# The third chunk of x with seven block products: V's first tile and kv first, sums and low parts earlier

## The chip, the core and the metric

The kernel runs on one core of a Trainium2 chip. The engines have queues of their own, which run in program order and meet only through semaphores: TensorE (PE in the profile) multiplies, VectorE (DVE), ScalarE (ACT) and GpSimd (POOL) work on elements, and SyncE (SP) issues most of the DMAs. The metric is the device time of one execution in microseconds; several executions are timed and their median is taken. A second, profiled execution gives the trace.

## What is computed

x is 2048 x 512. Two branches work on it and a gate mixes them:

```python
g = sigmoid((x * gate_w).sum(-1, keepdims=True))
q, k, v = split_heads(x @ wqkv)                      # 32 heads of 16
phi(u)  = concat(softmax(u @ w_phi), softmax(-(u @ w_phi)))
kv, z   = phi(k)^T v, sum over rows of phi(k)
a = (phi(q) kv / (phi(q) z + 1e-6)) @ wo
b = mish(x @ w1 + b1) @ w2
out = g * a + (1 - g) * b
```

All is float32.

## The kernel before, in words

Every float32 operand of TensorE is split into a high part, rounded to the multiplier's format (a copy on ScalarE), and a low part, the rest (a subtraction on VectorE or GpSimd). A product then takes three matmuls: high by high, high by low, low by high.

**Stage A** goes through x in 8 chunks of 256 rows (c = 0 to 7, two tiles of 128 rows each). w_phi is multiplied into the weights of q and k first, so a chunk needs six products of 128 x 512 by 512 x 512: k, v and q of two tiles. Each is 12 matmuls (4 along the 512, times 3). The chunk gives phi(k), which VectorE and ScalarE make, kv is summed up in PSUM from phi(k) and v, and q goes to DRAM. **Stage B** then goes through 4 blocks of 512 rows with both branches; the two matrices of the Dense branch are loaded and split during stage A.

In the chunks of `FAST` (c = 3, 4, 5 before) the four products for k and q are made as a 2 x 2 block product in Strassen's manner (in Winograd's form): seven products of half the length, s1 to s7, of 6 matmuls each, in place of eight. It needs four sums of the weights, t1, t3, t2 and t4 (made once, from the raw weights, and split: steps h0 to h3 for the high parts, l0 to l3 for the low parts, numbered in this order), and four sums of quarters of x for each such chunk, step `sa` (four additions on GpSimd), split by `sh0`, `sh1` (ScalarE) and `sl0`, `sl1` (GpSimd). s7 takes the first sum of x and t3, s6 the second and t2, s5 the third and t1, s3 the fourth and a block of wq; s1, s2 and s4 take x itself. The pieces meet so: `bc` copies s1's result to a second PSUM tile (ScalarE), on which s6, s5 and s3 accumulate; `m7` copies s7's (ScalarE); `ca` adds m7 to that tile (VectorE) and starts the tile of k of the second 128 rows, on which s4 accumulates; `qa` makes q of the second tile (VectorE). So s4 waits for ca, ca for s6 and m7, and s6 for bc.

Other steps, by the names in the lists: `xh`, `xl` split the next chunk's x (ScalarE, VectorE); `ldx` loads the chunk after that one; `mx`, `mn` are the row maxima and minima of k per head, `d0`, `d1` the two differences, `E` the exponential, `S` its sums, `rS` their reciprocal, `ml` the scaled E = phi(k) (all on VectorE but E); a digit behind them is the tile. `ve` copies v out, `qe` q; `st` stores q. `z` adds phi(k) to a sum in DRAM by a DMA that GpSimd issues (directly on GpSimd from c = 5 on). `kk` is the kv product of two chunks (128 small matmuls), `kv` of one. `H`, `O`, `L` are the split (high, low) of a piece of the Dense branch's weights and the load of a later piece; `O` is on GpSimd.

The order is written out by hand, as a list of steps for each chunk (FIRST, SECOND, BEFORE, SEVEN, NEXT, LAST); a mark behind a name means the previous chunk ('), the next (+), or a step of the weights (#). Each engine runs its own instructions in the order of these lists. `behind(ins)` adds a wait: the GpSimd instruction starts only when VectorE's step noted last (`dve[0]`: an `xl`, an `ml`) is done. Buffers rotate: the raw x and the sums of x share two tiles (`tx`), k's PSUM tiles three (`a`), the others four (`dn`), v's tiles four (`io`).

In the list BEFORE, for chunk 2, the order on TensorE is k0, kk, k1, v0, v1, q0, q1. In SEVEN it is s1, s7, s2, (kk,) s6, v0, s4, s5, v1, s3; in the first of these chunks v1 and s3 stand ahead of E1. `run` reads a list. A step that has been run is gone from the table, so a name that comes a second time does nothing.

Of the kernel before, what the change touches and what calls it, by code (L numbers as in the profile page):

```python
# [12 lines left out]
ALU = mybir.AluOpType  # L13
# [18 lines left out]
GROW = FA % P  # L32
ORDER = [NFA - 1] + list(range(NFA - 1)) + list(range(NFA, NF))
WARM = 6
FAST = range(3, 6)

# [3 lines left out]
    S0 rS0 ml0 S1 rS1 ml1 q0 qe0 st0 q1 qe1 st1  # L42
"""
SECOND = """
    h0# h1# l0# z0' z1' k0 mx0 mn0 d00 d10 ldx k1 E0 L0# L1# xh mx1 mn1 d01 d11 v0 E1 S0 rS0 ve0 ml0 xl z0
    v1 S1 rS1 ml1 ve1 q0 qe0 st0 q1 qe1 st1 t2#
"""
BEFORE = """
    z1' xh xl k0 kk h3# l1# mx0 mn0 d00 d10 k1 E0 sa ldx sh0 sl0 sh1 sl1 h2# mx1 mn1 d01 d11 v0 E1 H0# O0# L2# l2# S0 rS0 ve0 ml0 z0
    v1 H1# S1 rS1 ml1 l3# O1# L3# ve1 q0 qe0 st0 q1 qe1 st1  # L50
"""
SEVEN = """
    s1 bc ve1' s7 m7 sh1' sl1' s2 kk xh xl zld sa z1' more mx0 s6 ca mn0 d00 d10 E0 ldx v0 ve0 sh0 sl0 za rest S0 rS0 s4 s5 qa st1 mx1 mn1 d01 d11 E1 ml0 late
# [41 lines left out]
def tile_gated_mix(ctx: ExitStack, tc: tile.TileContext, xT, wv, wkT, wqT, bd, w1a, w1b, b1, w2a, w2b, wo, out):  # L95
# [6 lines left out]
    pin = tc.keep_in_program_order  # L102
    SYNC = mybir.DependencyInfo(mybir.DependencyClass.Sync, mybir.DependencyReason.DATA)
    V, G_, A_, Sy = nc.vector, nc.gpsimd, nc.scalar, nc.sync
# [11 lines left out]
    def k4(name, tag, dt=F32):  # L116
        return T([P, 1024], dt, tag, {"E": 4, "tx": 2, "oh": 2, "z": 1}[tag], name)
# [8 lines left out]
    def act(out_, in_, fn=AF.Copy, **k):  # L126
        return pin(A_.activation(out_, in_, fn, **k))  # L127

    def kt(t, f):
        return t[:, : KT * f].rearrange("p (k f) -> p k f", f=f)  # L130
# [4 lines left out]
    def f32(ap):  # L135
        return ap.bitcast(F32)
# [65 lines left out]
    def at(key, name, fn):  # L202
        steps.setdefault((key, name), []).append(fn)

    def run(text, key, prev=None, nxt=None):
        for w in text.split():
            k = prev if w.endswith("'") else nxt if w.endswith("+") else "W" if w.endswith("#") else key
            for fn in steps.pop((k, w.rstrip("'+#")), ()):
                fn()
# [4 lines left out]
    xs, Es, vs, psA, low = {}, {}, {}, {}, {}  # L214
# [41 lines left out]
    def feat_ops(key, t, src, d, negative=False):  # L256

        n = str(t)

        def red(name, op):  # L260
            d[name] = T([P, H], F32, name, 2, name)
            pin(V.tensor_reduce(d[name], hv(src()), axis=AX.X, op=op))

        def dd(a):
            if "E" not in d:
                d["E"] = k4("E", "E")
            E = hv(d["E"][:, a * 512 : (a + 1) * 512])
            if (a == 0) != negative:
                pin(V.tensor_sub(E, hv(src()), d["mx"][:, :, None].to_broadcast([P, H, DH])))
            else:  # L270
                ins = pin(V.tensor_sub(E, d["mn"][:, :, None].to_broadcast([P, H, DH]), hv(src())))  # L271
                if key[0] == "B":
                    dve[0] = ins

        def ss():
            d["S"] = T([P, 2 * H], F32, "Sm", 2, "Sm")
            pin(V.tensor_reduce(d["S"], hv(d["E"][:, :]), axis=AX.X, op=ALU.add))  # L277

        at(key, "mx" + n, lambda: red("mx", ALU.max))
        at(key, "mn" + n, lambda: red("mn", ALU.min))  # L280
        at(key, "d0" + n, lambda: dd(0))
        at(key, "d1" + n, lambda: dd(1))
        at(key, "E" + n, lambda: act(d["E"], d["E"], AF.Exp))
        at(key, "S" + n, ss)
        at(key, "rS" + n, lambda: pin(V.reciprocal(d["S"], d["S"])))

    dve = {}

    def behind(ins, other=None):
        tc.add_manual_dep(ins.ins, (other or dve[0]).ins.name, SYNC, reason="VectorE's step first")  # L290

    def scale_by(d, eng):
        dve[0] = pin(eng.tensor_mul(hv(d["E"][:, :]), hv(d["E"][:, :]), d["S"][:, :, None].to_broadcast([P, 2 * H, DH])))  # L293
# [6 lines left out]
    SX = [t[:, 1024:2048].rearrange("p (i k f) -> p i k f", i=4, k=2) for t in TS]  # L300
    SR = []

    def tops():

        k0, k1, q0, q1 = raw = [x[:, i : i + 2, :] for x in (wkr, wqr) for i in (0, 2)]
        t1, t4, t3, t2 = raw
        hl = [(*(x[:, i, :, :] for i in range(3)), y) for x, y in zip(TT, T4)]
        at("W", "t1", lambda: pin(G_.tensor_sub(t1, k0, q0)))
        at("W", "t3", lambda: pin(G_.tensor_sub(t3, q1, q0)))
        at("W", "t4", lambda: pin(G_.tensor_sub(t4, q1, k1)))  # L310
        at("W", "t4", lambda: pin(G_.tensor_add(t4, t4, t1)))
        at("W", "t2", lambda: pin(V.scalar_tensor_tensor(t2, t1, -1.0, q1, op0=ALU.mult, op1=ALU.subtract)))
        for i, r in enumerate((t1, t3, t2, t4)):
            at("W", f"h{i}", lambda i=i, r=r: act(hl[0][i], r))
            if i in (1, 3):
                at("W", f"l{i}", lambda i=i, r=r: behind(pin(G_.tensor_sub(hl[1][i], r, f32(hl[0][i])))))
            else:
                at("W", f"l{i}", lambda i=i, r=r: pin((V if i else G_).tensor_sub(hl[1][i], r, f32(hl[0][i]))))
        return list(zip(*hl))

    (t1, t3, t2, t4) = tops()
    wk0, wk1, wq1 = (wkh[:, :2, :], wkl[:, :2, :]), (wkh[:, 2:, :], wkl[:, 2:, :]), (wqh[:, 2:, :], wql[:, 2:, :])

    def kt4(t):
        return [t[:, o : o + 512].rearrange("p (i k f) -> p i k f", i=2, k=2) for o in (0, 512)]

    def fast_operands(c, key):

        def sa():
            SR[:] = kt4(k4("sraw", "tx"))  # L330
            r = kt(rawx[c], SC)
            a11, a12, a21, a22 = [r[:, k : k + 2, t * P : (t + 1) * P] for t in range(2) for k in (0, 2)]
            (s3, s2), (s1, s4) = [[x[:, i, :, :] for i in range(2)] for x in SR]
            for o, a, b in ((s1, a21, a22), (s3, a11, a21), (s2, a11, s1), (s4, a12, s2)):
                ins = pin(G_.tensor_add(o, a, b))
                if o is s1:
                    behind(ins, low[c])

        at(key, "sa", sa)
        for j in range(2):  # L340
            sl = slice(2 * j, 2 * j + 2)
            at(key, f"sh{j}", lambda j=j, sl=sl: act(SX[0][:, sl, :, :], SR[j]))
            at(key, f"sl{j}", lambda j=j, sl=sl: pin(G_.tensor_sub(SX[1][:, sl, :, :], SR[j], f32(SX[0][:, sl, :, :]))))

    def fast_ops(c, key, P_):

# [47 lines left out]
    def a_ops(c):  # L394
        key = ("A", c)
        P_ = psA[c] = {}
        for t in range(2):
# [28 lines left out]
            at(key, f"v{t}", v_)  # L426
            if c not in FAST:
                at(key, f"k{t}", k_)
                at(key, f"q{t}", q_)
            at(key, f"ve{t}", ve)  # L430
            if t and c in FAST:
                at(key, "qa", qa)
            else:
                at(key, f"qe{t}", qe)
            at(key, f"st{t}", st)
            feat_ops(key, t, lambda t=t: P_["k", t][:, :], d, t == 1 and c in FAST)
            at(key, f"ml{t}", lambda d=d: scale_by(d, V))

            def zs(t=t, d=d):
                if c >= FAST[-1]:  # L440
                    for sl in (slice(0, 512), slice(512, 1024)) if t and c == NCH - 1 else (slice(0, 1024),):
                        behind(pin(G_.tensor_add(Z["acc"][:, sl], Z["acc"][:, sl], d["E"][:, sl])))
                elif c:
                    pin(G_.dma_start(zd[t][:, :], d["E"], accum_op=ALU.add))
                else:
                    pin(G_.dma_start(zd[t][:, :], d["E"]))

            at(key, f"z{t}", zs)
        if c == FAST[-1]:
            def zld():  # L450
                Z["acc"] = k4("zacc", "z")
                pin(Sy.dma_start(Z["acc"], zd[0][:, :]))
# [17 lines left out]
        odd = c + 1 - c % 2  # L470
        if c <= FAST[-1]:
            at(("A", odd + 1), "kk", kv)
# [4 lines left out]
        if c + 1 in FAST:  # L477
            fast_operands(c + 1, key)
# [13 lines left out]
    W = {}  # L492
# [349 lines left out]
    for j in range(2):  # L842
        h, l = [w[:, 2 * j : 2 * j + 2, :].rearrange("p k f -> p (k f)") for w in (wvh, wvl)]
# [12 lines left out]
    for i in range(4):  # L856
        j, r = i // 2, i % 2
# [13 lines left out]

    run(FIRST, ("A", 0))
    run(SECOND, ("A", 1), ("A", 0))
    run(BEFORE, ("A", 2), ("A", 1))
    for c in FAST:
        w = {3: ("", "H2# O2# L4# H3#", "O3# L5# z0"), 4: ("", "H4# O4# L11# H5#", "O5# L7# z0"), 5: ("H11# O11# L8# H7# O7# L9#", "", "H8# O8# L6#")}[c]
        text = SEVEN
        for name, part in zip(("more", "rest", "late"), w):
            text = text.replace(name, part)
        if c == FAST[0]:  # L880
            text = text.replace("E1 ml0", "v1 s3 qe0 st0 E1 ml0").replace("v1 S1 rS1 s3 ve1 qe0 st0 ml1", "S1 rS1 ml1")
        run(text, ("A", c), ("A", c - 1))
    for c, text in ((NCH - 2, NEXT), (NCH - 1, LAST)):
        run(text, ("A", c), ("A", c - 1), ("B", 0))
# [63 lines left out]
```

## Time and profile before

| | |
|---|---|
| median of 3 runs | 449.17 us (449.09 to 449.27) |
| the profiled execution: its time, and its span | 449.46 us, 447.7 us |
| TensorE's granted clock | 1.0 |
| chunk 2 on TensorE (k0 to q1) | 46.66 to 65.13 us |
| chunk 3 on TensorE (s1 to s3) | 65.13 to 80.09 us |
| stage A ends, stage B begins | 149.4 us |

How the profile is read: a row of the timeline has the start in us from the span's start, the duration in us, the engine, the line of the program, the operation, the tiles (written <- read, by the program's names without buffer numbers), their sizes, the count that is merged in the row, and in brackets the time the engine had waited just before, with what ended the wait. Many rows have line 107 (every matmul) or 127 (every ScalarE copy), since helpers issue them; so the tiles tell the steps apart: `proj<-w2ah,w2bh` is a block product of sums (s7, s6 or s5), `proj<-w2bh,xh` is s4, since the weights' sums lie in tiles named w2a and w2b until the Dense branch's weights take their place. The sums of x have the name `sraw`, and their split lies in w2bh and w2bl. A matmul's recorded duration overlaps that of the next one; start to start tells the pace.

### The profile page before, as it was taken

What the parts mean: (1) busy time and instruction counts of PE and PEld (TensorE: products, weight loads), DVE (VectorE), ACT (ScalarE), POOL (GpSimd) and SP (SyncE); (2) the same over time, 40 slices, a digit from 0 to 9 for tenths busy, and PEclk for the clock granted to TensorE, in tenths of its full rate; (3) what the DMA queues carried; (4) which work ended last, traced back from release to release, by engine and by line L of the source; (5) the groups of instructions that cost most, each with busy time, mean ns of one, the idle gap of its engine ahead of it and who ended that gap; (6) DMA issues with size and microseconds to landing.
All of it is one profiled execution on the core that took longest, in us unless ns stands there. A gap on an engine that the chain in (4) does not pass through costs nothing.

```text
span 447.7 us, 7013 instructions
## 1 busy us (share of the span) xinstructions
PE 441.1 (99%) x2754; PEld 360.8 (81%) x2754; DVE 318.5 (71%) x423; ACT 209.4 (47%) x289; POOL 157.7 (35%) x116
## 2 busy tenths in 40 slices
PE   7999999999999999999999999999999999999996
PEld 7888888888888888787787887887887888787885
DVE  2499787988999999699979867386967529701002
ACT  4774454464545746426365443634253544233220
POOL 2296657775558263312022221113212123221211
PEclk9999999999999999999999999999999999999999
DMA  7426746869934200405352141321141302030002
GB/s 281 167 66 220 145 120 162 209 145 267 289 135 130 72 24 14 128 9 130 111 156 69 48 141 47 93 97 47 42 147 49 88 7 94 1 89 7 0 0 94
DMA packets 27320, 46.35 MB, mean 104 GB/s; under 512 B 5908, under 2 KB 14100, under 8 KB 27288
## 3 DMA queue, kind: packets, MB, share of 16 engines
q1 hardware_dynamic: 25528, 39.88, 28.9%
q0 software_dynamic: 1616, 5.77, 6.7%
q8 instruction: 21, 0.34, 0.3%
q10 hardware_dynamic: 144, 0.26, 0.2%
q14 instruction: 11, 0.09, 0.1%
HBM read 23.87 MB, written 13.64 MB: 84 GB/s over the span
## 4 chain that ended last, share of the span: by engine, by line
PE 98%; DMA 1%; DVE 0%; issue 0%
PE proj L107 29%; PE up L107 27%; PE down L107 26%; PE wo L107 10%; PE num L107 2%; PE fuse L107 2%; PE kvp L107 2%; DMA bds<-in_bd_dram 1%; DVE io L787 0%; PE z L107 0%; PE kvT L606 0%
## 5 line engine op out<-in xcount | busy, mean ns | idle before, releaser
L652 POOL TENSOR_TENSOR l<-act,h 128x512 fp32r<-128x512 f32 x44 | 60.8, 1384 | 220.2 <-ACT h L127 183.8
L127 ACT ACTIVATE act<-up,b1s 128x512 f32<-128x512 f32 x44 | 30.3, 689 | 89.0 <-PE up L107 85.2
L127 ACT ACTIVATE E<-E 128x1024 f32<-128x1024 f32 x32 | 33.6, 1060 | 52.8 <-DVE E L271 32.8
L293 DVE TENSOR_TENSOR E<-E,Sm 128x1024 f32<-128x1024 f32 x32 | 45.9, 1435 | 1.0
L277 DVE TENSOR_REDUCE Sm<-E 128x64 f32<-128x1024 f32 x32 | 38.7, 1211 | 6.3 <-ACT E L127 6.3
L107 PE MATMUL wo<-woh,ohl 128*128 128x512 f32 x128 | 40.8, 389 | 0.0
L107 PE MATMUL down<-w2ah,h 128*128 128x512 f32 x96 | 37.5, 390 | 0.0
L107 PE MATMUL down<-w2ah,l 128*128 128x512 f32 x96 | 37.4, 389 | 0.0
L107 PE MATMUL down<-w2al,h 128*128 128x512 f32 x96 | 37.4, 389 | 0.0
L787 DVE SCALAR_TENSOR_TENSOR io<-down,og_sb,io 128x512 f32<-128x512 f32 x16 | 11.1, 749 | 31.0 <-PE down L107 31.0
L107 PE MATMUL down<-w2bh,h 128*128 128x512 f32 x80 | 31.2, 390 | 0.0
L107 PE MATMUL down<-w2bl,h 128*128 128x512 f32 x80 | 31.1, 389 | 0.0
L107 PE MATMUL down<-w2bh,l 128*128 128x512 f32 x80 | 31.1, 389 | 0.0
L127 ACT ACT_TABLE_LOAD x20 | 25.7, 1283 | 10.1 <-PE up L107 9.8
L761 DVE TENSOR_TENSOR ohl<-num,ohl 128x512 fp32r<-128x512 f32 x16 | 10.2, 679 | 26.4 <-ACT ohl L127 26.4
L127 ACT ACTIVATE h<-act 128x512 fp32r<-128x512 f32 x44 | 27.8, 632 | 1.4
L107 PEld LDWEIGHTS wo<-woh,ohl 128*128 128x128 f32 x128 | 24.0, 188 | 5.1
L107 PE MATMUL up<-xbh,w1ah 128*128 128x512 f32 x96 | 26.2, 394 | 0.0
L107 PE MATMUL up<-xbh,w1al 128*128 128x512 f32 x96 | 25.7, 389 | 0.0
L107 PE MATMUL up<-xbl,w1ah 128*128 128x512 f32 x96 | 25.7, 389 | 0.0
L107 PE MATMUL wo<-wol,ohl 128*128 128x512 f32 x64 | 24.9, 389 | 0.0
L549 DVE TENSOR_TENSOR xbl<-xraw,xbh 128x1024 fp32r<-128x1024 f32 x8 | 10.0, 1288 | 19.8 <-ACT xbh L127 19.8
(156 smaller groups left out, 1007.3 us busy)
## 6 DMA issues: line engine op xcount, KB each, us to landing
xraw<-in_xT_dram SPq DMA_DIRECT2D x16, 512.0 KB, 4.4
eT<-tt SPq DMA_DIRECT2D x128, 64.0 KB, 2.0
zd<-E POOLq DMA_DIRECT2D x10, 512.0 KB, 6.4
pqd<-qs SPq DMA_DIRECT2D x16, 256.0 KB, 3.9
pq<-pqd SPq DMA_DIRECT2D x16, 256.0 KB, 2.9
out_dram<-io SPq DMA_DIRECT2D x16, 256.0 KB, 2.1
raw<-in_w1a_dram SPq DMA_DIRECT2D x3, 512.0 KB, 4.6
raw<-in_w2a_dram SPq DMA_DIRECT2D x3, 512.0 KB, 4.0
```

Source lines behind the costliest of these rows:

```text
L107: return pin(nc.tensor.matmul(*a, **k))
L127: return pin(A_.activation(out_, in_, fn, **k))
L277: pin(V.tensor_reduce(d["S"], hv(d["E"][:, :]), axis=AX.X, op=ALU.add))
L293: dve[0] = pin(eng.tensor_mul(hv(d["E"][:, :]), hv(d["E"][:, :]), d["S"][:, :, None].to_broadcast([P, 2 * H, DH])))
L549: dve[0] = pin(V.tensor_sub(xb[b][1][:, :, sl], kt(raw[h], SC), f32(xb[b][0][:, :, sl])))
L652: pin(G_.tensor_sub(U[i]["l"], U[i]["a"], f32(U[i]["h"])))
L761: pin(V.tensor_sub(ohl[h, gp][:, 512:], num[h, gp], f32(ohl[h, gp][:, :512])))
L787: pin(V.scalar_tensor_tensor(io[t], dn[t], og_sb[:, i : i + 1], io[t], op0=ALU.mult, op1=ALU.add))
```

## The change

The chunks with seven products are c = 2 to 5 now. For that, the list of chunk 2 is a new one (THIRD), some steps of chunk 1's list (SECOND) are added or moved, and three more orders are changed. The diff, cut:

```diff
-FAST = range(3, 6)
+FAST = range(2, 6)
...
 SECOND = """
-    h0# h1# l0# z0' z1' k0 mx0 mn0 d00 d10 ldx k1 E0 L0# L1# xh mx1 mn1 d01 d11 v0 E1 S0 rS0 ve0 ml0 xl z0
-    v1 S1 rS1 ml1 ve1 q0 qe0 st0 q1 qe1 st1 t2#
+    h0# h1# l0# z0' z1' k0 mx0 mn0 d00 d10 k1 E0 L0# L1# xh mx1 mn1 d01 d11 v0 E1 S0 rS0 ve0 sa ml0 xl sh0 sl0 z0 ldx
+    v1 S1 rS1 ml1 ve1 q0 qe0 st0 q1 qe1 st1 t2# sh1
 """
-BEFORE = """
-    z1' xh xl k0 kk h3# l1# mx0 mn0 d00 d10 k1 E0 sa ldx sh0 sl0 sh1 sl1 h2# mx1 mn1 d01 d11 v0 E1 H0# O0# L2# l2# S0 rS0 ve0 ml0 z0
-    v1 H1# S1 rS1 ml1 l3# O1# L3# ve1 q0 qe0 st0 q1 qe1 st1
+THIRD = """
+    z1' l1# h3# h2# l2# l3# v0 kk ve0 H0# xh xl sl1' s1 bc sa s7 m7 H1# s2 mx0 mn0 s6 ca d00 d10 E0 ldx sh0 sl0 v1 O0# L2# O1# L3# ve1
+    S0 rS0 s4 s5 qa st1 mx1 mn1 d01 d11 s3 qe0 st0 E1 ml0 z0 S1 rS1 ml1
 """
...
+        def t2_():
+            dve[0] = pin(V.scalar_tensor_tensor(t2, t1, -1.0, q1, op0=ALU.mult, op1=ALU.subtract))
+
+        def l2_():
+            dve[0] = pin(V.tensor_sub(hl[1][2], t2, f32(hl[0][2])))
...
-                if o is s1:
+                if o is s1 and c in low:
                     behind(ins, low[c])
...
+            def sl_(j=j, sl=sl):
+                ins = pin(G_.tensor_sub(SX[1][:, sl, :, :], SR[j], f32(SX[0][:, sl, :, :])))
+                if c == FAST[0]:
+                    behind(ins)
...
-    run(BEFORE, ("A", 2), ("A", 1))
-    for c in FAST:
+    run(THIRD, ("A", 2), ("A", 1))
+    for c in FAST[1:]:
...
-        if c == FAST[0]:
+        if c == FAST[1]:
+            text = text.replace("s2 kk xh xl", "s2 xh s6 ca xl")
             text = text.replace("E1 ml0", "v1 s3 qe0 st0 E1 ml0").replace("v1 S1 rS1 s3 ve1 qe0 st0 ml1", "S1 rS1 ml1")
+        if c == FAST[2]:
+            text = text.replace("s2 kk", "s2").replace("s6 ca", "s6 kk ca")
```

Read by engine: chunk 2's k0, k1, q0 and q1 on TensorE become s1 to s7, behind v0 and kk. Chunk 1's list now has `sa`, `sh0`, `sl0` and `sh1` of chunk 2's sums of x, and loads the raw x of chunk 3 later (`ldx`). t2 and l2 on VectorE are now steps that a GpSimd step can be put behind: l1 is behind t2, l3 behind l2, `sl0` and `sl1` of chunk 2's sums behind the latest `xl`. In chunk 3, `ca` comes ahead of `xl` on VectorE; in chunk 4, kk comes after s6 on TensorE.

More of the change, by code (lines that the diff above doesn't have):

```diff
@@ L44 @@
 SECOND = """
-    h0# h1# l0# z0' z1' k0 mx0 mn0 d00 d10 ldx k1 E0 L0# L1# xh mx1 mn1 d01 d11 v0 E1 S0 rS0 ve0 ml0 xl z0
-    v1 S1 rS1 ml1 ve1 q0 qe0 st0 q1 qe1 st1 t2#
-"""
-BEFORE = """
-    z1' xh xl k0 kk h3# l1# mx0 mn0 d00 d10 k1 E0 sa ldx sh0 sl0 sh1 sl1 h2# mx1 mn1 d01 d11 v0 E1 H0# O0# L2# l2# S0 rS0 ve0 ml0 z0
-    v1 H1# S1 rS1 ml1 l3# O1# L3# ve1 q0 qe0 st0 q1 qe1 st1
+    h0# h1# l0# z0' z1' k0 mx0 mn0 d00 d10 k1 E0 L0# L1# xh mx1 mn1 d01 d11 v0 E1 S0 rS0 ve0 sa ml0 xl sh0 sl0 z0 ldx
+    v1 S1 rS1 ml1 ve1 q0 qe0 st0 q1 qe1 st1 t2# sh1
+"""
+THIRD = """
+    z1' l1# h3# h2# l2# l3# v0 kk ve0 H0# xh xl sl1' s1 bc sa s7 m7 H1# s2 mx0 mn0 s6 ca d00 d10 E0 ldx sh0 sl0 v1 O0# L2# O1# L3# ve1
+    S0 rS0 s4 s5 qa st1 mx1 mn1 d01 d11 s3 qe0 st0 E1 ml0 z0 S1 rS1 ml1
 """
@@ L311, in tops @@
         at("W", "t4", lambda: pin(G_.tensor_add(t4, t4, t1)))
-        at("W", "t2", lambda: pin(V.scalar_tensor_tensor(t2, t1, -1.0, q1, op0=ALU.mult, op1=ALU.subtract)))
+        def t2_():
+            dve[0] = pin(V.scalar_tensor_tensor(t2, t1, -1.0, q1, op0=ALU.mult, op1=ALU.subtract))
+        def l2_():
+            dve[0] = pin(V.tensor_sub(hl[1][2], t2, f32(hl[0][2])))
+        at("W", "t2", t2_)
+        at("W", "l2", l2_)
         for i, r in enumerate((t1, t3, t2, t4)):
@@ L316, in tops @@
                 at("W", f"l{i}", lambda i=i, r=r: behind(pin(G_.tensor_sub(hl[1][i], r, f32(hl[0][i])))))
-            else:
-                at("W", f"l{i}", lambda i=i, r=r: pin((V if i else G_).tensor_sub(hl[1][i], r, f32(hl[0][i]))))
+            elif not i:
+                at("W", "l0", lambda r=r: pin(G_.tensor_sub(hl[1][0], r, f32(hl[0][0]))))
         return list(zip(*hl))
@@ L342, in fast_operands @@
             at(key, f"sh{j}", lambda j=j, sl=sl: act(SX[0][:, sl, :, :], SR[j]))
-            at(key, f"sl{j}", lambda j=j, sl=sl: pin(G_.tensor_sub(SX[1][:, sl, :, :], SR[j], f32(SX[0][:, sl, :, :]))))
+            def sl_(j=j, sl=sl):
+                ins = pin(G_.tensor_sub(SX[1][:, sl, :, :], SR[j], f32(SX[0][:, sl, :, :])))
+                if c == FAST[0]:
+                    behind(ins)
+            at(key, f"sl{j}", sl_)
     def fast_ops(c, key, P_):
```

## The prediction

> **What bounds the kernel now.** I read the page's busy times first, then TensorE's list of waits.
>
> ```profile
> span 447.7 us, 7013 instructions
> PE 441.1 (99%) x2754; PEld 360.8 (81%) x2754; DVE 318.5 (71%) x423; ACT 209.4 (47%) x289; POOL 157.7 (35%) x116
> ...
> PE fuse L107 <- DMA bds<-in_bd_dram: 1.7, 1, 1.7
> PE warm L107 <- DVE ones L175: 1.1, 1, 1.1
> ```
>
> TensorE waits twice, at the start, and never again: each matmul taken away is a gain as long as nothing makes it wait. So the question is who is close behind it. TensorE's timeline, then VectorE's:
>
> ```profile
> 46.66 1.07 PE L107 MATMUL proj<-wkh,xh 128*128 128x512 f32 x4
> 49.47 1.99 PE L107 MATMUL kvp<-E,v 128*32 128x64 f32 x128
> 65.13 0.62 PE L107 MATMUL proj<-wkh,xh 128*128 128x512 f32 x2
> 73.29 0.62 PE L107 MATMUL proj<-w2bh,xh 128*128 128x512 f32 x2
> 80.09 0.62 PE L107 MATMUL proj<-wkh,xh 128*128 128x512 f32 x2
> 90.39 0.62 PE L107 MATMUL proj<-w2bh,xh 128*128 128x512 f32 x2
> 105.35 0.62 PE L107 MATMUL proj<-w2bh,xh 128*128 128x512 f32 x2
> ...
> 72.07 0.68 DVE L381 TENSOR_TENSOR proj<-proj,m 128x512 f32<-128x512 f32 x1
> 88.11 0.68 DVE L381 TENSOR_TENSOR proj<-proj,m 128x512 f32<-128x512 f32 x1
> 104.28 0.68 DVE L381 TENSOR_TENSOR proj<-proj,m 128x512 f32<-128x512 f32 x1
> ```
>
> The first two rows are chunk 2's k0 and kk; 65.13 and 80.09 are s1 of chunks 3 and 4; 73.29, 90.39 and 105.35 are s4 of chunks 3, 4 and 5, and the rows of VectorE are the `ca` that s4 waits for. ca ends 0.5, 1.6 and 0.4 us ahead of s4 (73.29 less 72.75, 90.39 less 88.79, 105.35 less 104.96). VectorE is a near second bound, and its margin is less than the gain that the change is after.
>
> Why VectorE is slow there is seen beside GpSimd:
>
> ```profile
> 41.45 1.22 DVE L293 TENSOR_TENSOR E<-E,Sm 128x1024 f32<-128x1024 f32 x1
> 42.59 1.28 DVE L254 TENSOR_TENSOR xl<-xraw,xh 128x512 fp32r<-128x512 f32 x2
> 68.00 2.39 POOL L516 TENSOR_TENSOR w1al<-raw,w1ah 128x1024 fp32r<-128x1024 f32 x1
> 69.24 2.30 DVE L254 TENSOR_TENSOR xl<-xraw,xh 128x512 fp32r<-128x512 f32 x2 [3.69 <-ACT xh L127]
> 81.80 2.41 POOL L516 TENSOR_TENSOR w1bl<-raw,w1bh 128x1024 fp32r<-128x1024 f32 x1 [1.43 <-ACT qs L127]
> 83.76 1.53 DVE L293 TENSOR_TENSOR E<-E,Sm 128x1024 f32<-128x1024 f32 x1
> 84.74 1.69 POOL L343 TENSOR_TENSOR w2bl<-sraw,w2bh 128x512 fp32r<-128x512 f32 x1
> 85.21 2.38 DVE L254 TENSOR_TENSOR xl<-xraw,xh 128x512 fp32r<-128x512 f32 x2
> 88.06 1.44 POOL L335 TENSOR_TENSOR sraw<-xraw 128x256 f32<-128x256 f32 x2 [1.62 <-issue]
> ```
>
> Alone, an `ml` takes 1.22 us and a pair of `xl` 1.28. Beside GpSimd the pair at 69.24 ends at 71.54, 1.15 after GpSimd's end (70.39); the `ml` at 83.76 ends at 85.29, 1.08 after 84.21; GpSimd's step from 84.74 ends 1.14 after that ml; the next xl ends at 87.59, 1.16 after GpSimd's 86.43. One waits for the other's whole instruction, and the one that asked first goes first. VectorE's steps on PSUM don't wait (ca at 88.11 takes its 0.68 beside the additions at 88.06), nor do its reductions (S at 81.92, shown below, takes 1.22 beside 81.80).
>
> **The change part by part.** The sum is made against the profiled execution (449.46 us, of it 447.7 span; what lies around it I leave alone) and carried over to the median, 449.17.
>
> *TensorE.* Eight products of 6 matmuls become seven. Chunk 3 took 14.96 us for 66 matmuls (80.09 less 65.13), 0.2267 each: six fewer are **-1.36 us**. Without stalls v0 runs from 46.66 to 49.4, kk to 51.5 with the gaps around it, s7 begins at 52.9 and s4 at 59.7; chunk 3 begins at 63.77, s5 of chunk 2 ends at 62.41, and s4 of chunks 3, 4 and 5 begins at 71.93, 89.03 and 103.99. v0 and kk ahead of s1 cost nothing: their inputs are chunk 1's and older, and they give l1 and l2 some 5 us of cover. kk behind s6 in chunk 4 covers 1.36 us of ml1 and costs nothing either.
>
> *ScalarE* loses one `qe`, gains bc, m7, and makes sh0 and sh1 of one chunk more: some 0.6 us each, hidden by its 53% of idle time. It decides once, below.
>
> *The sums of chunk 2 in chunk 1.* Rows for GpSimd's pieces:
>
> ```profile
> 39.46 1.13 POOL L446 DMA_DIRECT2D zd<-E  x2
> 43.20 0.89 POOL L444 DMA_DIRECT2D zd<-E  x1 [2.60 <-DVE E L293]
> 47.38 0.88 POOL L444 DMA_DIRECT2D zd<-E  x1 [3.29 <-DVE E L293]
> 51.80 1.43 POOL L335 TENSOR_TENSOR sraw<-xraw 128x256 f32<-128x256 f32 x2
> 53.19 1.54 POOL L335 TENSOR_TENSOR sraw<-xraw,sraw 128x256 f32<-128x256 f32 x2
> 54.70 2.54 POOL L343 TENSOR_TENSOR w2bl<-sraw,w2bh 128x512 fp32r<-128x512 f32 x2
> ...
> 46.77 1.22 DVE L312 SCALAR_TENSOR_TENSOR wqr<-wkr,wqr 128x1024 f32<-128x1024 f32 x1
> ```
>
> `sa` is four additions, 2.93 us (51.80 to 54.73), from 40.6, when GpSimd has issued z0 and z1. VectorE asks for ml0 at 41.45 and then for two xl: with turns taken it gets ml0 from 42.0, and the last xl ends at 45.7, not 43.87. Bounds: 0 to 2.9 later; I take 1.8, as the turns give. t2 ends at 49.85, not 47.99. TensorE doesn't notice: kk wants ml1 at 50.9 (it starts at 49.5 and comes to that quarter last).
>
> *GpSimd in chunk 2.* l1 behind t2, 50.0 to 52.4 (2.39 like L516); l2 on VectorE then, to 53.5; first half of xl; l3, behind l2, 54.0 to 56.4; second half, to 56.95; `sl1` behind it, 1.27, to 58.35 (queued behind it: sa, sl0, O0 and O1; nobody waits for the first two yet); sa of chunk 3 to 61.25; sl0, once E0 and sh0 are through ScalarE, to 62.95; O0 and O1, 2.39 each, to **67.7**. Each weight is in time: l1 for s7 at 53.3, l3 for s4 at 59.7. L2 and L3 on SP's queue wait for O0 and O1, so the two `st` behind them go at about 68 instead of 63; the next user of those buffers is qa at 79.
>
> *VectorE in chunk 2.* s5 ends at 62.41, S0 and rS0 at about 62.8, whichever is last. From there I go by chunk 3's rows:
>
> ```profile
> 77.39 0.63 DVE L420 SCALAR_TENSOR_TENSOR qs<-proj,m 128x512 f32<-128x512 f32 x1
> 80.45 1.22 DVE L293 TENSOR_TENSOR E<-E,Sm 128x1024 f32<-128x1024 f32 x1
> 81.92 1.22 DVE L277 TENSOR_REDUCE Sm<-E 128x64 f32<-128x1024 f32 x1 [0.25 <-ACT E L127]
> ```
>
> qa to ml0 is 3.06, so ml0 asks at 65.9. O1 holds the port until 67.7: 1.8 lost. ml0 ends at 68.75. From S1 to ml1 is 1.84 (81.92 to 83.76), so ml1 asks at 70.5. GpSimd meanwhile issues z0 (0.5 after ml0 by the rows at 43.20 and 47.38, some 0.6 for the issue) and starts chunk 3's `sl1` at about 69.8, to 71.1; ml1 ends at 72.2, ca at 72.8. TensorE is ready for s4 at 71.93: **+0.85**. Had neither port wait come, ca would end at 70.8. Bounds for these two waits: 0 to 2.39 and 0 to 1.29.
>
> *Chunks 3 to 5.* The xl after ca is undisturbed (GpSimd's sa is behind it), and mx0 comes at 73.85 with ca done, where before it came at 71.47 with ca (0.60) to follow: VectorE is 1.8 us late. What follows is a chain of its own steps with the same port waits as before.
>
> ```profile
> 80.83 1.05 ACT L127 ACTIVATE E<-E 128x1024 f32<-128x1024 f32 x1
> 81.78 0.59 ACT L127 ACTIVATE proj<-proj 128x512 f32<-128x512 f32 x1
> ...
> 101.78 1.98 DVE L254 TENSOR_TENSOR xl<-xraw,xh 128x512 fp32r<-128x512 f32 x2 [0.96 <-ACT xh L127]
> ```
>
> The second row is chunk 4's bc, queued behind E1. The last difference of chunk 3 ended at 80.5 and will at 82.3; E1 and bc to 83.9; s6 of chunk 4, now without kk ahead of it, is ready at 82.81 + 0.85 = 83.65: **+0.3**. ml1 ends at 87.0 (O3, then the port), where kk comes to its last quarter at 86.8: **+0.25**. ca of chunk 4 ends at 88.79 + 1.7 = 90.5, and s4 is ready at 90.43: **+0.15**. Before chunk 5's xl VectorE had 0.96 us to spare, of which the delay of 1.7 eats most: xl ends at 104.75, not 103.76, ca at 105.95, s4 is ready at 105.53: **+0.5**. Sum: -1.36 + 0.85 + 0.3 + 0.25 + 0.15 + 0.5 = **+0.7 us**.
>
> *After that* VectorE, 1.0 late, has hardly a gap up to stage B's first transposes:
>
> ```profile
> 176.48 10.25 SPq L740 DMA_DIRECT2D eT<-tt  x16
> 188.25 1.25 DVE L720 STREAM_TRANSPOSE tt<-E 128x1024 f32<-128x1024 f32 x1 [3.27 <-DMA eT<-tt]
> 189.09 1.02 PE num L107 x32
> ```
>
> The transfers have landed by 188.25, when VectorE may write `tt` again, and the product follows at 189.09: 0.8 of margin. VectorE 1.0 and TensorE 0.7 late leave 0.5: no stall there.
>
> [...] The row at 47.38 shows z1's issue beside t2 (46.77 to 47.99) in 0.88 us, as at 43.20. [...]
>
> **The rivals.**
>
> *All is covered: -1.36, 447.8 us.* It takes ca of chunk 3 by 71.9, hence no more than 1.1 us of port waits after qa, where I count 2.3, and VectorE on time until chunk 5. For it: 0.96 us to spare there, and 3.69 before chunk 3's xl; against it, most of the latter is spent by chunk 2's two added steps and its later end.
>
> *ml0 goes ahead of O1: -0.3, 448.9 us.* If GpSimd is 0.6 us later than I count, O0 ends when ml0 already asks. VectorE wins 0.95 net (O1 and sl1 then stand before ml1 and xl), s4 of chunk 3 doesn't wait, and ca of chunk 5 ends at 105.0 against 103.99: -1.36 + 1.05. Every hop of a semaphore that I took too short works for it.
>
> *`sl1` takes its whole 1.29 us from ml1: slower, +1.4, 450.6 us.* I have it start at 69.8, with 0.7 run when ml1 asks at 70.5, so it costs 0.55. Starting between 69.8 and 70.5 it costs up to 0.75 more, and all of chunk 3 to 5 is later by that. From 70.0 on it carries the time past +0.9; from 70.5 ml1 goes first and this turns into a gain of 0.5. For it: z0's issue, just ahead, has rows of 0.57 to 0.89. Against it: the window is half a microsecond.
>
> **How the numbers follow.** Two kernels are told apart here at 0.2%, 0.9 us. My sum: 0.37, at 449.17 + 0.7 = 449.85. ml0 first: 0.15. All covered, or nearly: 0.15. Slower by the whole of sl1, or by another such turn among some ten: 0.33. My sum and ml0 first lie within 0.9 us: 0.52 for no change; 0.15 faster, 0.33 slower. The range goes from 448.2, where most of full cover is left out, to 450.7, just past the slow rival; the forecast's own is 449.3 to 450.3.
>
> **What would show it.** The five stalls would stand as gaps before s4 of chunk 3, s6, kk's last quarter and s4 of chunk 4, and s4 of chunk 5, the first the longest; ml0 of chunk 2 would be recorded at 2.8 us and end 1.1 after O1. If TensorE's list of waits is as short as before and stage B begins at 148.0, full cover holds and I am wrong on VectorE. Gaps at other places, s7 or s5 of chunk 2 above all, would mean that a low part is late, which I rule out. If the matmuls of chunk 2 are 66 and the span does not move, the gain was given back where I say; a stall at the product at 189 would mean that VectorE's delay grew after stage A.

## The result, and the profile after

| | before | after |
|---|---|---|
| median (6 runs each, beside each other) | 448.96 us (448.79 to 449.27) | 450.62 us (449.69 to 450.95) |
| ratio | | 1.0034 (1.0021 to 1.0047) |
| profiled execution: time, span | 449.46, 447.7 us | 450.85, 449.1 us |
| first kk to Stage B's first matmul | 99.85 us | 101.53 us |

The changed kernel is slower: 0.34% by the ratio, 1.66 us between the medians. 449.85 was forecast with a range to 450.7, and "slower" had a chance of 0.33. The size is at the far end of the range, and the places of the loss are not those forecast.

The page of after, and TensorE's list of waits (what ended them: total us, times, longest):

```profile
span 449.1 us, 7018 instructions
PE 440.2 (98%) x2748; PEld 358.4 (80%) x2748; DVE 325.5 (72%) x425; ACT 210.9 (47%) x292; POOL 164.6 (37%) x122
...
PE fuse L107 <- DMA bds<-in_bd_dram: 1.9, 1, 1.9
PE proj L107 <- DVE qs L434: 1.8, 2, 1.1
PE warm L107 <- DVE ones L175: 1.1, 1, 1.1
PE proj L107 <- issue: 0.2, 1, 0.2
```

Six matmuls fewer, as the change says (2754 to 2748), and 0.9 us less busy; but two lines are new, a wait for `qs`, twice, and one for "issue". Stage B's first matmul before, where the distance from kk ends:

```profile
149.32 1.20 PE L107 MATMUL up<-xbh,w1ah 128*128 128x512 f32 x4
```

TensorE's timeline after has three places where time is lost (start, duration, in brackets the wait before):

```profile
48.97 1.99 PE L107 MATMUL kvp<-E,v 128*32 128x64 f32 x128
...
61.45 0.61 PE L107 MATMUL proj<-w2ah,w2bl 128*128 128x512 f32 x2
62.85 0.74 PE L107 MATMUL proj<-wqh,w2bh 128*128 128x512 f32 x2 [0.78 <-DVE qs L434]
...
72.57 0.62 PE L107 MATMUL proj<-w2bh,xh 128*128 128x512 f32 x2
...
77.10 1.07 PE L107 MATMUL proj<-wvh,xl 128*128 128x512 f32 x4
79.22 0.73 PE L107 MATMUL proj<-wqh,w2bh 128*128 128x512 f32 x2 [1.05 <-DVE qs L434]
...
86.28 1.99 PE L107 MATMUL kvp<-E,v 128*32 128x64 f32 x128
88.20 0.73 PE L107 MATMUL proj<-wvh,xh 128*128 128x512 f32 x2
89.17 0.73 PE L107 MATMUL proj<-wvh,xh 128*128 128x512 f32 x2 [0.23 <-issue]
...
150.50 1.20 PE L107 MATMUL up<-xbh,w1ah 128*128 128x512 f32 x4
```

Start to start, at 0.2267 us for a matmul, the gaps are: before s3 of chunk 2, 0.95 (62.85 less 61.45 less two matmuls); before s3 of chunk 3, 1.21; inside v0 of chunk 4, 0.52. The first pair behind each takes 0.12 or 0.13 more than its pace (the rows of 0.73 in place of 0.62). Together 3.05; of that 0.11 is a slow pair right behind kk, which before has as well, so 2.94 is new. With the six matmuls, -1.36 + 2.94 = +1.58, and the distance from kk to Stage B grew by 101.53 - 99.85 = 1.68. So these three gaps are nearly all of the lost time; the other 0.1 lies in no single place. s4 of chunk 3, where the first and longest stall was forecast, follows without a wait.

What holds s3: it accumulates on the PSUM tile of q, and `qa` has to read that tile between s5 and s3 (to make q of the second 128 rows). VectorE of after (S0, rS0, qa; then ml0, ml1, ca; then qa of chunk 3), and GpSimd beside it:

```profile
60.26 1.22 DVE L277 TENSOR_REDUCE Sm<-E 128x64 f32<-128x1024 f32 x1 [1.13 <-ACT E L127]
61.52 0.55 DVE L285 RECIPROCAL Sm<-Sm 128x64 f32<-128x64 f32 x1
62.10 0.69 DVE L434 SCALAR_TENSOR_TENSOR qs<-proj,m 128x512 f32<-128x512 f32 x1
...
65.23 2.68 DVE L293 TENSOR_TENSOR E<-E,Sm 128x1024 f32<-128x1024 f32 x1
...
69.66 1.84 DVE L293 TENSOR_TENSOR E<-E,Sm 128x1024 f32<-128x1024 f32 x1
71.42 0.69 DVE L395 TENSOR_TENSOR proj<-proj,m 128x512 f32<-128x512 f32 x1
...
76.82 1.22 DVE L277 TENSOR_REDUCE Sm<-E 128x64 f32<-128x1024 f32 x1 [1.13 <-ACT E L127]
78.07 0.55 DVE L285 RECIPROCAL Sm<-Sm 128x64 f32<-128x64 f32 x1
78.54 0.63 DVE L434 SCALAR_TENSOR_TENSOR qs<-proj,m 128x512 f32<-128x512 f32 x1
```

```profile
62.08 4.75 POOL L530 TENSOR_TENSOR w1al<-raw,w1ah 128x1024 fp32r<-128x1024 f32 x2
68.20 0.88 POOL L458 DMA_DIRECT2D zd<-E  x1 [1.38 <-DVE E L293]
68.80 1.60 POOL L353 TENSOR_TENSOR w2bl<-sraw,w2bh 128x512 fp32r<-128x512 f32 x1
```

In chunk 2 s5's last pair starts at 61.45 and TensorE is free about 61.9; VectorE is then busy with the reciprocal, qa ends at 62.79, s3 starts at 62.85. In chunk 3 qa ends at 79.17 and s3 starts at 79.22. The turns with GpSimd stand where they were forecast: ml0 waits for O1 (62.08 + 4.75 = 66.83; ml0 ends at 67.91, 1.08 later), and ml1 takes 1.84 beside `sl1`.

### The profile page after: what moved, and what is told of

It is laid out like the page before. It is cut to its first block, busy times and chain, and to the rows that moved or that the text cites. A ratio compares the mean times of both kernels' runs of the same rounds, so it can differ in the third digit from the quotient of the medians.

```text
span 449.1 us, 7018 instructions
## 1 busy us (share of the span) xinstructions
PE 440.2 (98%) x2748; PEld 358.4 (80%) x2748; DVE 325.5 (72%) x425; ACT 210.9 (47%) x292; POOL 164.6 (37%) x122
## 4 chain that ended last, share of the span: by engine, by line
PE 94%; DVE 3%; DMA 1%; issue 1%; ACT 0%; DVEq 0%
PE up L107 27%; PE down L107 26%; PE proj L107 25%; PE wo L107 10%; PE num L107 2%; PE kvp L107 2%; PE fuse L107 2%; DMA bds<-in_bd_dram 1%; DVE E L293 1%; DVE Sm L277 1%; DVE io L801 0%; DVE E L271 0%; DVE mx L262 0%; DVE mn L262 0%; DVE E L269 0%
## 5 line engine op out<-in xcount | busy, mean ns | idle before, releaser
L293 DVE TENSOR_TENSOR E<-E,Sm 128x1024 f32<-128x1024 f32 x32 | 48.2, 1507 | 1.0
```

## The experiments

In the expectations, A is the theory of the paragraph above: VectorE's chain, late by its own order and by its turns with GpSimd, reaches qa too late, and s3 waits. F is that the gap in v0 is TensorE's supply of instructions. B, C, D and G are rivals, told where they are used. Eight to twelve executions were timed for each of e1 to e8, and the kernel before ran beside them (449.24, 449.07 and 449.09 us in the three groups). The intervals are some 0.6 us to either side, so the main measure is the profile: the distance from the first kk to Stage B's first matmul, and the gaps in it (start to start, in us; of each gap in v0 0.11 is the slow pair that before has too).

| kernel | median us | ratio to before | distance | s3, chunk 2 | s3, chunk 3 | v0, chunk 4 | other |
|---|---|---|---|---|---|---|---|
| before | 449.1 | 1 | 99.85 | - | - | - | - |
| after | 450.62 | 1.0034 | 101.53 | 0.95 | 1.21 | 0.52 | - |
| e0, after again | 451.84, one | - | 101.78 | 0.95 | 1.23 | 0.72 | - |
| e1, qa first in chunk 3 | 450.56 | 1.0030 | 101.92 | 0.95 | - | 1.50 | 0.67, s2 of chunk 4 |
| e2, v1 split | 450.70 | 1.0032 | 101.99 | 0.81 | 1.39 | 0.91 | - |
| e3, O1 behind ml0 | 450.38 | 1.0013 | 101.16 | 0.95 | 0.24 | 1.09 | - |
| e4, a load later | 450.43 | 1.0026 | 101.08 | 0.95 | 1.25 | - | - |
| e5 = e1 + e3 + e4 | 449.28 | 0.9995 | 99.77 | 0.95 | - | - | - |
| e6 = e5 + v1 split, qa ahead of rS0 | 448.47 | 0.9989 | 99.49 | 0.27 | - | - | 0.27, s2 of chunk 3 |
| e6 again | 448.81 | 0.9997 | 99.61 | 0.30 | - | - | 0.25, s2 of chunk 3 |
| e7 = after + v1 split, qa ahead of rS0 | 450.96 | 1.0038 | 101.54 | 0.24 | 1.49 | 0.52 | 0.28, s2 of chunk 3 |
| e8 = e6 + l3 behind xl | 448.58 | 0.9994 | 99.31 | - | - | - | 0.27, s2 of chunk 3 |

**e0: the changed kernel once more.**

> The changed kernel itself, profiled once more. Theory A (VectorE's chain of steps in chunks 2 and 3 is the bound; TensorE waits for it at s3, which may not add to a PSUM tile before qa has read it): the same two gaps, 0.8 to 1.0 us at chunk 2's s3 and 1.1 to 1.3 at chunk 3's. The gap of half a microsecond inside chunk 4's v0, which nothing in the first profile releases: if it belongs to this order of instructions it comes again at the same matmul; if it is chance it is gone or elsewhere.

Both gaps at s3 recur to 0.02 us, and v0 stops again behind its first two matmuls: none is an accident of one profile. (A gap of 0.41 in Stage B, for `xbh` of ScalarE, is seen here, at 0.25 to 0.44 in e3, e4 and e5, and at 0.11 in after, not in before; e6 again has one of 0.49 for `xbl` of VectorE. They stay open, and lie outside the distance.)

**e1: qa ahead of the sums in chunk 3.**

```diff
+            text = text.replace("S0 rS0 s4 s5 qa st1", "s4 s5 qa st1 S0 rS0")
```

> In chunk 3 alone, qa stands ahead of S0 and rS0 on VectorE, in the 1.1 us in which VectorE waits for E0. Theory A: the 1.2 us gap before chunk 3's s3 goes, with the slow restart after it; the time falls by 1.0 to 1.35 us against the changed kernel, to 449.3 to 449.6. Rival B (what VectorE is late by comes out at its next step that TensorE needs, ca or ml1): the gap moves to s6, kk or s4 of chunks 4 and 5, and the time stays within 0.4 us of 450.6.

TensorE's waits:

```profile
PE proj L107 <- issue: 1.2, 1, 1.2
...
PE proj L107 <- DVE qs L434: 0.8, 1, 0.8
PE proj L107 <- ACT proj L127: 0.5, 1, 0.5
```

One of the two waits for qs is gone, as A says, so it was that wait. The time isn't gained. ScalarE's second exponential of chunk 3, `bc` of chunk 4 behind it, and TensorE's next step:

```profile
81.61 1.06 ACT L127 ACTIVATE E<-E 128x1024 f32<-128x1024 f32 x1 [0.93 <-DVE E L269]
82.58 0.58 ACT L127 ACTIVATE proj<-proj 128x512 f32<-128x512 f32 x1
...
83.21 0.74 PE L107 MATMUL proj<-wkh,xh 128*128 128x512 f32 x2 [0.50 <-ACT proj L127]
```

Counted from kk, TensorE is ready for s2 of chunk 4 1.35 us earlier than in after, but the exponential starts only 0.57 earlier. bc ends at 83.16, and s2, which accumulates on s1's tile that bc has to read, waits 0.67 for it. The forecast's second stall had the same cause, bc behind the exponential, but stood one product later, at s6; in after TensorE was late enough itself not to meet it. The rest is taken by v0's gap, which grew to 1.50. Ratio 1.0030 (1.0014 to 1.0045): no gain.

**e2: the last third of v1 (4 matmuls of 12) between s5 and s3 of chunk 2**, as cover for qa. `proj` may now stop after two of its three parts; `vend` runs the third.

```diff
...
-... ldx sh0 sl0 v1 O0# L2# O1# L3# ve1
-    S0 rS0 s4 s5 qa st1 mx1 mn1 d01 d11 s3 qe0 ...
+... ldx sh0 sl0 v1 O0# L2# O1# L3#
+    S0 rS0 s4 s5 qa st1 vend ve1 mx1 mn1 d01 d11 s3 qe0 ...
...
```

> In chunk 2 alone, the last 4 of v1's 12 matmuls stand between s5 and s3 instead of ahead of s4, so that TensorE has 0.9 us of work while qa runs. Theory A: the first gap (0.8 us) goes, and the gap before chunk 3's s3 grows by as much, since VectorE is no earlier there; the time is unchanged, within 0.3 us of 450.6. Rival C (each gap adds by itself): 0.9 us faster, 449.7.

A miss: the gap in chunk 2 stays, 0.81 for 0.95. VectorE and TensorE:

```profile
59.96 1.22 DVE L279 TENSOR_REDUCE Sm<-E 128x64 f32<-128x1024 f32 x1 [1.13 <-ACT E L127]
61.21 0.55 DVE L287 RECIPROCAL Sm<-Sm 128x64 f32<-128x64 f32 x1
61.68 0.63 DVE L439 SCALAR_TENSOR_TENSOR qs<-proj,m 128x512 f32<-128x512 f32 x1
```

```profile
60.65 1.07 PE L107 MATMUL proj<-wvh,xl 128*128 128x512 f32 x4
62.37 0.73 PE L107 MATMUL proj<-wqh,w2bh 128*128 128x512 f32 x2 [0.65 <-DVE qs L439]
```

s5 is done when v1's last four matmuls start (60.65), but qa comes at 61.68 all the same, since VectorE is still at S0 and rS0. The work ahead of s3 is as much as before, only in another order. What has to move is qa, not s5.

**e3: O1 behind ml0 on GpSimd in chunk 2.**

```diff
-... v1 O0# L2# O1# L3# ve1
-    ... s3 qe0 st0 E1 ml0 z0 S1 rS1 ml1
+... v1 O0# L2# ve1
+    ... s3 qe0 st0 E1 ml0 O1# L3# z0 S1 rS1 ml1
```

> In chunk 2 alone, the low part O1 on GpSimd stands behind ml0 instead of ahead of it. Theory A: ml0 takes 1.2 us, not 2.7; ml1 then waits for the end of O1 by about 0.6; VectorE reaches ca of chunk 3 some 1.2 earlier and qa of chunk 3 some 0.5 to 0.9 earlier, so the second gap shrinks from 1.2 to 0.3 to 0.7 us; time 449.7 to 450.1. Rival D (the port wait only moves from ml0 to ml1 and to xl): qa of chunk 3 at the same time, 450.6.

VectorE's ml0, ml1 and chunk 3's qa:

```profile
65.89 1.22 DVE L293 TENSOR_TENSOR E<-E,Sm 128x1024 f32<-128x1024 f32 x1
...
68.94 1.72 DVE L293 TENSOR_TENSOR E<-E,Sm 128x1024 f32<-128x1024 f32 x1
...
78.21 0.63 DVE L434 SCALAR_TENSOR_TENSOR qs<-proj,m 128x512 f32<-128x512 f32 x1
```

ml0 takes 1.22 in place of 2.68. This trace lies 0.66 later than after's at ml0 (65.89, 65.23), so ml0 ends 1.46 and qa of chunk 3 0.99 earlier in the schedule, and the gap at s3 of chunk 3 falls from 1.21 to 0.24. The wait for O1 was 1 us of that gap. The distance falls only 0.37, as v0's gap goes up by 0.57; the ratio is 1.0013 (0.9999 to 1.0028).

**e4: the load L4 waits for O3** in chunk 3, on SP's queue behind the q stores.

```diff
...
+            if j == 4:
+                tc.add_manual_dep(last[0].ins, lows[3].ins.name, SYNC, reason="after O3")
...
-        w = {3: ("", "H2# O2# L4# H3#", "O3# L5# z0"),
+        w = {3: ("", "H2# O2# H3#", "O3# L4# L5# z0"),
```

> The load L4 (512 KB, a piece of the Dense branch's weights) waits for O3, so it is issued after 85 us instead of at 81.5. Theory F: the gap in chunk 4's v0 (0.5 to 1.5 us in the five profiles of the changed order) is TensorE out of instructions: kk runs through 256 of them in 2 us, the block behind them is fetched by DMA, and its packet stands behind L4 and the two stores of q; with L4 later the packet starts at about 83 to 84 instead of 86.7 to 87.6, and the gap goes: 0.6 to 0.8 us faster than the changed kernel. Rival G (v0's third matmul waits for something of the computation, a buffer or a split): the gap stays where it is, at half a microsecond or more, and so does the time.

The reason for it is in the DMA queues. The page has a queue of the kind "instruction" (q8) with 21 packets, 0.34 MB, which is taken to bring TensorE's: there are 5496 matmuls and weight loads, 262 for each packet. kk is 128 matmuls and 128 weight loads in 2 us, about one packet's worth. A block is what one packet brings. The times below are counted from one record of TensorE, the same in each kernel (79.86 in before, where the packet runs 0.9 us later; 82.08 in after, 82.81 in e4). It is called the block's end here; that a block ends there, and that the packet in question is asked for there, is an assumption, since the trace shows only when the packet ran. Queue, packets, MB, share of the 16 DMA engines, first before from 80 to 81 us, then after from 85 to 86, after from 86 to 87, and e4 from 85 to 86:

```profile
q0 software_dynamic: 52, 0.15, 78.1%
q8 instruction: 1, 0.02, 5.9%
```

```profile
q1 hardware_dynamic: 171, 0.38, 97.8%
```

```profile
q1 hardware_dynamic: 144, 0.26, 79.2%
q8 instruction: 1, 0.02, 5.5%
```

```profile
q8 instruction: 1, 0.02, 6.0%
```

In after, SP issues L4 (512 KB) and two q stores around the block's end:

```profile
81.53 0.33 SPq L165 DMA_DIRECT2D raw<-in_w1b_dram  x1
81.96 1.04 SPq L438 DMA_DIRECT2D pqd<-qs  x2
```

The packets of q1 alone take 97.8% of the DMA engines' time from 85 to 86 us, and the packet runs at 86.72, 4.6 us after the block's end; in before it took 0.9 us, in e4 2.8. v0's third matmul, due at 88.77 by its pace, starts at 89.17. With the load later, e4 passes there without a gap:

```profile
86.98 1.99 PE L107 MATMUL kvp<-E,v 128*32 128x64 f32 x128
88.90 1.20 PE L107 MATMUL proj<-wvh,xh 128*128 128x512 f32 x4
```

So the load makes this gap: it is gone in e4 and in the four other runs that hold the load back (e5, e6 twice, e8), and stands in all six without (after, e0, e1, e2, e3, e7), each time before v0's third matmul, and each time TensorE goes on 1.2 to 1.6 us after the packet has ended. G, which had the gap stay, falls. The two gaps at s3 stay, 0.95 and 1.25, so they are of another cause. That TensorE lacks this packet's instructions, and that the packet stands behind the load in the same engines' queues, is read from the times; a packet was not tried by itself. Nor does the time of the load's issue settle it alone: it was 0.5 us ahead of the block's end in after and 0.9 us behind it in e1, where the packet was the latest (6.4 us after the end), but 0.5 us behind it in before, where the packet ran first. What decides between these two stays open.

**e5: e1, e3 and e4 together.**

> Three edits together: O1 behind ml0 in chunk 2, qa ahead of S0 in chunk 3, L4 after O3. Theory A with F: only the gap before chunk 2's s3 is left (0.95 and 0.13 for the restart): against the kernel before, -1.36 + 1.08 = -0.3 us, that is 0.1 us on either side of its time by what a run can tell. Rival B (VectorE's lateness comes out elsewhere): gaps of 0.5 us or more at s6, kk or s4 of chunks 4 and 5; 0.5 us or more slower than before.

Only the gap of chunk 2 is left in the stage; distance 99.77, ratio 0.9995 (0.9983 to 1.0007). The interval lies clear of after's (1.0021 to 1.0047). Alone, none of the three came to that: with e1 or e3 TensorE came earlier and met v0's longer gap, with e1 bc as well, and e4 left both gaps at s3.

**e6: e5, with v1 split and qa between S0 and rS0 in chunk 2.**

```diff
...
-    S0 rS0 s4 s5 qa st1 mx1 mn1 d01 d11 s3 qe0 st0 E1 ml0 O1# L3# z0 S1 rS1 ml1
+    S0 s4 s5 qa st1 rS0 vend ve1 mx1 mn1 d01 d11 s3 qe0 st0 E1 ml0 O1# L3# z0 S1 rS1 ml1
```

> The three edits, and in chunk 2 the last 4 matmuls of v1 between s5 and s3, with qa between S0 and rS0: s5 then ends 0.9 us sooner, and qa runs 0.6 sooner on VectorE. Theory A with F: the gap before chunk 2's s3 falls to 0.2 to 0.4; -1.36 + 0.4 = -0.9 to -1.0 us against the kernel before. Rival B: a gap of 0.5 us or more opens at s4 of chunk 3 (waiting for ca) or behind it, and the time stays within 0.4 of the run with three edits.

```profile
PE fuse L107 <- DMA bds<-in_bd_dram: 1.5, 1, 1.5
PE warm L107 <- DVE ones L177: 1.1, 1, 1.1
```

TensorE's list of waits is as short as in before. Two gaps of 0.27 are left; the second is s2 of chunk 3, which accumulates on the tile that `bc` has still to read, behind E1. Distance 99.49, ratio 0.9989 (0.9977 to 1.0000).

**e7: the same edit of chunk 2 on the changed kernel, without the others.**

> Of these, only the edit of chunk 2 (v1's last 4 matmuls between s5 and s3, qa between S0 and rS0), with O1, chunk 3's qa and L4 as in the changed kernel. Theory A: chunk 2's gap falls from 0.95 to 0.3, and the one before chunk 3's s3 grows by the same 0.6, since VectorE comes to chunk 3's qa no sooner: time within 0.3 us of the changed kernel. Rival C (the gaps add): 0.6 to 0.7 us faster than it.

```profile
61.41 0.73 PE L107 MATMUL proj<-wqh,w2bh 128*128 128x512 f32 x2
...
78.51 0.72 PE L107 MATMUL proj<-wqh,w2bh 128*128 128x512 f32 x2 [1.33 <-DVE qs L439]
```

The gap before s3 of chunk 2 goes from 0.95 to 0.24, and the distance stays at 101.54 for 101.53: chunk 3's gap takes 0.28 of it and s2 0.28 (with a slow first pair behind it). Counted from kk (48.23 here), ml0 ends at 18.96 for 18.94, since it waits for O1 all the same, and chunk 3's qa starts at 29.60 for 29.57. The gaps are not losses that add up; VectorE's chain sets where TensorE is by then, and TensorE waits for it at one place or the next.

**e8: e6, with l3 behind xl in chunk 2's list.**

```diff
-    z1' l1# h3# h2# l2# l3# v0 kk ve0 H0# xh xl sl1' s1 bc ...
+    z1' l1# h3# h2# l2# v0 kk ve0 H0# xh xl l3# sl1' s1 bc ...
```

> The six edits of e6_plus_v1_split's order, and in the third list the rest of the weights' low parts (l3, GpSimd, 2.8 us in the changed kernel) is called behind xl in place of ahead of xh. Theory (VectorE's order and its turns with GpSimd set what is left): xl of chunk 3, which took 3.5 us beside l3 in the changed kernel, takes 2.1 to 2.5; the maximum, the sums and q of chunk 2 come 0.3 to 0.7 us sooner, the gap of 0.27 us before chunk 2's s3 goes, and that of 0.27 before chunk 3's s2 stays or shrinks; the distance from the first kv product to the first up product goes from 99.49 to 99.0 to 99.3, and the time is 0.2 to 0.5 us below that of e6_plus_v1_split: ratio to before 0.997 to 0.998. Rival (the turns only move to the next pair, l3 beside the sums of chunk 2): no gap goes, the distance stays within 0.1 of 99.49 and the ratio at 0.999.

```profile
53.17 1.28 DVE L258 TENSOR_TENSOR xl<-xraw,xh 128x512 fp32r<-128x512 f32 x2
55.81 0.69 DVE L266 TENSOR_REDUCE mx<-proj 128x32 f32<-128x512 f32 x1 [1.35 <-PE proj L107]
```

The pair of xl takes 1.28 in place of 3.50 in e6 (2.1 to 2.5 was expected; it now runs alone), and VectorE then waits for TensorE; the gap before s3 of chunk 2 goes and that before s2 of chunk 3 stays, as expected. The distance is 99.31. The time is 0.23 below that of e6 beside it, which these intervals don't tell from nothing, and the ratio of 0.9994 (0.9982 to 1.0007) is not the 0.997 to 0.998 that was expected.

**e6 again.**

> The kernel of e6_plus_v1_split once more, beside the run with l3 behind xl. Theory: two gaps of 0.27 us and none else, a distance of 99.4 to 99.6 us, and a ratio to before of 0.998 to 1.000; if it is the faster order by what its gaps left out say (0.3 us of 449), the two intervals together lie below 1.000.

The gaps and the distance are as expected, the ratio is 0.9997 (0.9984 to 1.0010). By the condition that was set, e6 is not shown to be faster than before. What is shown: with the order mended, seven products in chunk 2 cost nothing against before that these timings show; a gain, 0.2 to 0.5 us by the distance, is less than these timings tell apart. Of the 1.36 us of TensorE's work, e8 keeps 0.54: 0.27 goes at s2 and 0.12 or 0.13 each in three slow first pairs; the last 0.2 is not accounted for.

## Why the prediction was right and where it was wrong

*TensorE's six matmuls, -1.36*: right; the gaps explain the distance, to 0.1 us, only with that term.

*VectorE and the turns with GpSimd*: right, nearly to the step. After's trace lies 0.5 us earlier than before's (kk at 48.97, not 49.47); with that, ml0 asks at 65.7 (forecast 65.9), O1 ends at 67.3 (67.7), ml1 ends at 72.0 (72.2), ca of chunk 3 at 72.6 (72.8), and ml0 has its 2.68 (2.8) and ends 1.08 after O1 (1.1). e3 shows by taking it away that the O1 wait is real (1.46 us of ml0). The prediction and rival D speak of a port there; no run shows one, and what the runs show is the turns: ml0 takes 2.68 beside O1 and 1.22 without it.

*The place and size of the stalls*: wrong. The sum counted +0.85, +0.3, +0.25, +0.15 and +0.5, at s4, s6, kk and s4 twice. None of these five is there. The step that failed is "ca to 72.8. TensorE is ready for s4 at 71.93": it follows TensorE from s5 straight into s3 and on to chunk 3. The meetings were listed as s4 for ca, ca for s6 and m7, s6 for bc, and s3 for qa, though s3 accumulates on a tile that qa reads, was not among them. The forecast's own numbers would have had it: s5 ends at 62.41, S0 and rS0 at about 62.8, qa takes some 0.65, so s3 can't start before 63.45, 1.04 late (measured: 0.95 and the slow pair). In chunk 3 qa, 1.8 late as the forecast has VectorE, stands at 79.2 to 79.9 against an s3 that was ready at 78.2. In the kernel before, v1's 12 matmuls stand between s5 and s3 of chunk 3, 2.7 us; in the new list for chunk 2 v1 stands ahead of s4 and nothing covers qa. Once TensorE is 1 us late at s3, ca is in time for s4 and bc for s6: the later stalls are the same lateness, met earlier.

A second meeting of that kind was left out, s2 for bc. By the forecast's own times bc of chunk 4 ends at 83.9, and s2 is due at 82.81 - 1.36 + 0.85 = 82.30, so s2 would have waited 1.6 us; 0.3 was counted, at s6. In after the losses at s3 hide it; e1, e6, e7 and e8 show such waits, 0.25 to 0.67.

*The size*: 2.05 counted, 2.94 found. At s3 it is 2.16 + 0.25 for slow pairs = 2.41, near the 2.05; the other 0.53 is v0's gap, which no step of the forecast had. Its removal alone gives 0.45 of distance (e4). Two of the five terms were larger than the times they were taken from: s4 of chunk 4 at 90.43 for a ca that ends at 90.5 is 0.07, not 0.15, and a VectorE 1.7 late with 0.96 to spare is 0.74 late at chunk 5's xl, not 1.0, which makes the last term 0.25, not 0.5. With these two the sum would have been +0.4.

That the time lies within the range is in part luck. VectorE's lateness was real and of the forecast size, but the stalls that were counted did not come, and stalls that were not counted, one of them of another cause, add up to somewhat more.

*The rivals.* "All is covered" fell: 101.53, not 98.5. "ml0 ahead of O1" fell by 1.6 us (O1 ends at 66.83, ml0 asks at 65.23); with that order written into the list (e3), it brings 0.37. "`sl1` takes its whole 1.29" named 450.6, which is the time that came, but not by its mechanism: ml1 takes 1.84, 0.62 more than alone, and 0.55 was counted.

*GpSimd's DMA issue beside t2*: as in the row at 47.38. In after z1's issue, 48.34 to 49.22, has 0.88 us beside t2 (47.95 to 49.17); GpSimd is not later by it.

*The tests.* "First the longest, before s4 of chunk 3" failed. That low parts are in time held: no gap at s7 or s5. That the product at 189 doesn't stall held too: TensorE has no gap there.

## What to carry to other kernels

To cost a new order, list every place where TensorE meets another engine, also those where it accumulates further on a PSUM tile that someone has yet to read, and put a margin to each; the first with too little takes the loss, and the ones behind it look covered (here s3 of chunk 2 with 0.95, and s4 of chunk 3 without a wait). A wait taken away at one place shows up at the next as long as the late engine is no earlier (e7: the gap at s3 of chunk 2 from 0.95 to 0.24, the distance 101.54 for 101.53), so move what makes it late (here GpSimd's steps beside VectorE's) and measure a distance in the profile, not a single gap. If TensorE stops for "issue" after a burst of small matmuls, look at what the DMA engines carry just before (here q1 at 97.8% from 85 to 86 us, and with the load later, in e4, no gap).

## What was not expected of the hardware

That TensorE can run out of instructions is read from these traces; a packet of q8 brings some 260, if all 21 are TensorE's (5496 matmuls and weight loads). In the six runs with a 512 KB load issued within 0.9 us of a block's end, and two stores beside it, the packet ran 4.6 to 6.4 us after that end, and TensorE then stopped for 0.4 to 1.4 us in the middle of a product. In the five with the load 3.3 to 3.5 us behind the block's end it ran after 2.3 to 2.8 us, and TensorE didn't stop; nor did it in before, where the load came 0.5 us behind the end and the packet ran 0.9 us after it.

The second is how VectorE and GpSimd take turns: for some pairs of steps one waits for the other's whole instruction (xl 3.50 beside l3, 1.28 without it, in e6 and e8). That was read from before's profile already; e3 and e8 confirm it by taking the neighbour away (ml0 2.68 and 1.22, xl 3.50 and 1.28). The time lies within the step's own recorded duration (ml0 of after, at 65.23, with no wait ahead of it), so the rows show the two meeting where no wait for a semaphore is recorded; the description of the engines at the start has semaphores alone.
